# Fourier mixing and a hard-swish layer: folding the first units on VectorE, with later evictions and another order of the first weight pieces

## The chip, the cores and the metric

The kernel runs on one core of a Trainium2 chip. The metric is the device time of one execution, in microseconds (us). TensorE is called PE here, VectorE DVE, ScalarE ACT, GpSimd POOL and SyncE SP, as in the profile. POOL, SP and ACT each have a queue from which DMA transfers are requested; the transfers of all three run on the same 16 DMA engines.

## The reference

```python
# x: (8, 3008, 256), w_in: (256, 2048), w_out: (2048, 256), all float32 or cast to it
X = np.fft.fft(x, axis=1)
X = np.fft.fft(X, axis=2)
t = X.real.astype(np.float32).reshape(8 * 3008, 256)
h = t @ w_in                       # the weights come in as 64-bit floats
g = h * np.clip(h + 3.0, 0.0, 6.0) / 6.0
out = (g @ w_out).astype(np.float32)
```

The weights arrive in double precision. The kernel reads their words and turns them into float32 itself: the exponent through a small matrix product, the mantissa with integer operations, and a product of both.

## The kernel before

The 3008 positions are 47 x 64. A first stage (`unit_columns`, `unit_middle`) is a product over the 47, a second stage (`stage2_half`) one over the 64, and the transform over the 256 columns is folded into w_in (`fold_w_in`). Then come the two products of the layer (`mlp1`, `mlp2`) in chunks of up to 256 positions, with ACT and DVE doing the activation between them. The images are worked on in pairs. Everything after the first pair's start is prepared beside the layer's products, which keep PE busy.

The program order is written out by hand (a manual schedule); each engine runs its instructions in that order, and waits on semaphores.

**The start.** Before the layer can run, the first image goes through the first stage in four units, in the order `FIRST = [0, 1, 3, 2]`. A unit is a block of four slots of 256 columns. It has two halves (`part` 0 and 1): the block itself (tile `xt` of `hb.x`) and its mirrored partner (`hb.xr`). All eight tiles are fetched by POOL's indirect gathers, one after the other (L175, 512 KB each). To *fold* a half is to add and subtract columns j and 256 - j: the cosine columns are the sums, the sine columns the differences, and columns 0 and 128 (the centre) are copied. The result is the tile `y` (two buffers).

For units 0 and 1 DVE subtracts only the sine columns of the first half (`fold_columns`, L203) into a tile `sine`, and PE makes the sums itself by two products per quarter on the unfolded tile (`unit_by_pe`, L355). All other halves are folded by DVE (`fold_all`, L203 and L212), the centre being copied by DVE (L214) or ACT (L209). `unit_columns` (L347, L352) multiplies a folded half by the tables in `F`, four 64-column quarters side by side in the array; `unit_middle` (L335) does column 128. Both halves accumulate into two PSUM tiles `ps` and a slice `pt`.

`evict_first` (L360) copies a unit's four PSUM tiles to `z` on ACT (L365 to L367; the last one of unit 2 on DVE) and requests two stores `zd<-z` (L379) on SP's queue, the last of all on ACT's. `load_g_half` (L447) loads them back, turned, for the second stage.

**The weight pieces** are called 0, 1, 2, ... Piece j goes through `load_w` (the request, L769 and L774, tile `st`), `exponent_a` on ACT (L790, tile `PM`), `exponent_b` on PE (L804, with the matrix in `FI`, into `ex`), `exponent_c` on ACT (L807), `mantissa` on DVE (L815, L816, tile `top`), and `join` on DVE (L824, tile `wi`, or L830 into `G`). Pieces 0 and 1 are two transfers of 256 KB each; 0 is requested on SP's queue behind `FI`, 1 on ACT's queue after unit 0 has been evicted, 2 and 3 on POOL's queue behind the gathers and two tables. `fold_w_in` (L860) multiplies pieces 0 and 1 by the table `C` into `wps`.

`keep_awake` (L887) is a filler: a product of ones and zeros into a PSUM tile that nobody reads, 512 columns wide. There are four at the start and one behind `fold_w_in(0)`. `clear_table` (L917) is a long ACT copy that zeroes half of the table `T`; there are two.

Of the kernel before, what the change touches and what calls it, by code (L numbers as in the profile page):

```python
# [58 lines left out]
def kernel(  # L59
# [141 lines left out]
    def fold_columns(x, y, part, js, eng):  # L201
        far, near = x[0:PX - 1, js, D - 1:P:-1], x[0:PX - 1, js, 1:P]
        eng.tensor_tensor(y[:, js, P + 1:D], *((far, near) if part else (near, far)), op=AL.subtract)  # L203
        return near, far

    def fold_all(x, part, eng, steps=(slice(0, XC),), copy=None):
        y = ypool.tile([PX - 1, XC + 1, D], F32, tag="y", name="y")
        if copy:
            copy(y[:, 0:XC, 0:P + 1:P], x[0:PX - 1, :, 0:P + 1:P])  # L209
        for js in steps:  # L210
            near, far = fold_columns(x, y, part, js, eng)
            eng.tensor_tensor(y[:, js, 1:P], near, far, op=AL.add)  # L212
            if not copy:
                eng.tensor_copy(y[:, js, 0:P + 1:P], x[0:PX - 1, js, 0:P + 1:P])  # L214
        return y
# [93 lines left out]
    def rows(b):  # L309
        return slice(b * PB, b * PB + N1)  # L310
# [21 lines left out]
    def unit_middle(m, part, x, pt, open_, close):  # L332
        for i, h, js, slots, alone in quarters(m, part):
            t = (1 + part) if alone else (5, 7)[part]
            nc.tensor.matmul(pt[h][i * PB:(i + 1) * PB, js], table(t, h), x[rows(h), slots, P:P + 1], start=open_ and not alone, stop=close,  # L335
                             skip_group_check=True)

    def unit_columns(m, part, src, ps, to, fr, open_, close, only=None):
        for i, h, js, slots, alone in quarters(m, part):
            parts = [(to, fr)]  # L340
            if alone and (to.start or 0) <= P < to.stop - 1:
                parts = [(slice(0, P + 1), slice(0, P + 1)), (slice(P + 1, D), slice(P + 1, D))]
            for a, b in parts:
                t = (1 + part + 2 * (a.start > P)) if alone else (0, 6)[part]
                o = ps[h][i * PB:(i + 1) * PB, js, a]
                if only is None:
                    nc.tensor.matmul(o, table(t, h), src[rows(h), slots, b], start=open_ and not alone, stop=close, skip_group_check=True)  # L347
                    continue
                js_, sl = range(js.start, js.stop), range(XC)[slots]
                for jj, ss in zip(js_, sl):  # L350
                    if jj == only:
                        nc.tensor.matmul(ps[h][i * PB:(i + 1) * PB, jj:jj + 1, a], table(t, h), src[rows(h), ss:ss + 1, b],  # L352
                                         start=False, stop=close, skip_group_check=True)

    def unit_by_pe(m, part, x, sine, ps, open_):  # L355
        unit_columns(m, part, x, ps, slice(0, P + 1), slice(0, P + 1), open_, False)
        unit_columns(m, part, x, ps, slice(1, P), slice(D - 1, P, -1), False, False)
        unit_columns(m, part, sine, ps, slice(P + 1, D), slice(P + 1, D), False, False)

    def evict_first(hb, m, ps, pt):  # L360
# [6 lines left out]
        (nc.vector.tensor_copy if k == NM - 1 else nc.scalar.copy)(z[:, 1, :, 0:D], ps[1][0:PX])  # L367
# [391 lines left out]
    def load_w(j):  # L759
# [5 lines left out]
        if kind == "in":  # L765
            c0, c1 = in_columns(n, i)
            for h, cs in enumerate((slice(c0, c1 + P),) if n else (slice(c0, c0 + P), slice(c1, c1 + P))):
                nf = cs.stop - cs.start
                (nc.sync, nc.scalar, nc.gpsimd)[min(j, 2)].dma_start(  # L769
# [113 lines left out]
    def keep_awake(n, ps=None):  # L883
        if ps is None:
            ps = ps_d.tile([P, 2 * TB], F32, tag="d", name="awake")
        for i in range(n):
            nc.tensor.matmul(ps[:], ones[:], Z[:], start=True, stop=True)  # L887
# [65 lines left out]
    mantissa(0)  # L953
    clear_table(1)
    every = slice(0, D)

    def fold_unit(k, part):
        x = (hb.xr if part else hb.x).pop(FIRST[k])
        if k < 2 and part == 0:
            sine = cpool.tile([PX - 1, XC, D], F32, tag="c", name="sine")  # L960
            fold_columns(x, sine, 0, slice(0, XC), nc.vector)
            return x, sine
        steps = (slice(1, XC, 2), slice(0, XC, 2)) if k == NM - 1 and part else (slice(0, XC),)
        return x, fold_all(x, part, nc.vector, steps, nc.scalar.copy if k > 1 else None)
# [338 lines left out]
```

## Time and profile before

| | us |
|---|---|
| runs | 1934.41, 1934.05, 1938.8 |
| median | 1934.41 |
| profiled execution, in all | 1933.92 |
| span of its core, first to last instruction | 1932.2 |
| granted TensorE clock, mean over the span | 0.997 |
| PE busy | 1915.4 |
| DVE busy | 1425.0 |
| ACT busy | 679.3 |
| POOL busy | 1442.7 |

The time of an execution is its span and 1.7 us around it. A row of the timeline gives start, length, engine, line, operation, output and inputs with their shapes, how many instructions are merged, and in brackets how long the engine was idle before and what ended that. A row of the busy time by stretches gives the stretch and its length, then for each engine the busy time and the number of instructions, then the granted clock (1.00 is full speed), the share of the DMA engines' time and GB/s. A row of the groups gives line, engine, operation, forms and count, then the busy time and the mean ns of one, then the idle time before them with what ended it.

### The profile page before, as it was taken

What the parts mean: (1) busy time and instruction counts of PE and PEld (TensorE: products, weight loads), DVE (VectorE), ACT (ScalarE), POOL (GpSimd) and SP (SyncE); (2) the same over time, 40 slices, a digit from 0 to 9 for tenths busy, and PEclk for the clock granted to TensorE, in tenths of its full rate; (3) what the DMA queues carried; (4) which work ended last, traced back from release to release, by engine and by line L of the source; (5) the groups of instructions that cost most, each with busy time, mean ns of one, the idle gap of its engine ahead of it and who ended that gap; (6) DMA issues with size and microseconds to landing.
All of it is one profiled execution on the core that took longest, in us unless ns stands there. A gap on an engine that the chain in (4) does not pass through costs nothing.

```text
span 1932.2 us, 28221 instructions
## 1 busy us (share of the span) xinstructions
PE 1915.4 (99%) x9354; PEld 1650.8 (85%) x9354; DVE 1425.0 (74%) x2752; ACT 679.3 (35%) x1168; POOL 1442.7 (75%) x1653
## 2 busy tenths in 40 slices
PE   8999999999999999999999999999999999999998
PEld 5688888888988888888898888888899888888887
DVE  6877776677777777777787777777778777777777
ACT  6543333333333333333333333333333333333332
POOL 4597888896688778787678877878666667666765
PEclk9999999999999999999999999999999999999999
DMA  8431232311112222121111221121110101101000
GB/s 286 122 87 49 56 83 72 64 44 38 32 33 67 62 53 55 44 54 34 31 36 50 52 55 44 52 53 50 36 28 20 28 17 27 33 14 28 18 21 20
DMA packets 155592, 99.03 MB, mean 51 GB/s; under 512 B 122163, under 2 KB 137246, under 8 KB 155446
## 3 DMA queue, kind: packets, MB, share of 16 engines
q1 hardware_dynamic: 142582, 57.63, 12.4%
q0 software_dynamic: 11168, 38.51, 6.8%
q8 instruction: 73, 1.20, 0.3%
q10 hardware_dynamic: 1696, 1.10, 0.2%
q14 instruction: 73, 0.60, 0.1%
HBM read 59.87 MB, written 37.32 MB: 50 GB/s over the span
## 4 chain that ended last, share of the span: by engine, by line
PE 96%; DVE 2%; ACT 1%; DMA 0%; issue 0%; another core or an unknown queue 0%; SPq 0%; DVEq 0%; ACTq 0%
PE acc L661 57%; PE v L566 17%; PE u L566 16%; PE ps L514 2%; PE acc L641 1%; PE ps L287 1%; DVE a L617 1%; PE spare L860 1%; DVE s L575 0%; ACT t L614 0%; DVE o L722 0%; PE ps L475 0%; DVE u L598 0%; DMA st<-in_moe_w_in_dram 0%; PE wps L860 0%
## 5 line engine op out<-in xcount | busy, mean ns | idle before, releaser
L631 POOL TENSOR_TENSOR c<-a 128x512 f32<-128x512 f32 (+1 forms) x375 | 469.0, 1251 | 360.3 <-PE acc L661 310.5
L661 PE MATMUL acc<-c,G 128*128 128x256 f32 (+1 forms) x3008 | 697.2, 375 | 0.0
L614 ACT ACTIVATE t<-u,half 128x512 f32<-128x512 f32 (+1 forms) x384 | 260.5, 678 | 1144.2 <-DVE u L585 1062.4
L661 PEld LDWEIGHTS acc<-c,G 128*128 128x128 f32 x3008 | 565.3, 190 | 71.5 <-POOL c L631 0.4
L575 DVE SCALAR_TENSOR_TENSOR s<-qn,WN,u 128x256 f32<-128x256 f32 (+1 forms) x768 | 330.2, 471 | 339.3 <-PE u L566 336.7
L661 PE MATMUL acc<-a,G 128*128 128x256 f32 (+1 forms) x2256 | 541.7, 376 | 0.0
L661 PEld LDWEIGHTS acc<-a,G 128*128 128x128 f32 x2256 | 421.0, 189 | 73.6 <-issue 20.2
L566 PE MATMUL v<-q,W 127*128 127x256 f32 (+1 forms) x1536 | 389.2, 375 | 1.6 <-DVE a L617 1.3
L566 PE MATMUL u<-q,W 128*128 128x256 f32 (+1 forms) x1536 | 387.9, 375 | 0.0
L617 DVE SCALAR_TENSOR_TENSOR a<-t,u 128x512 f32<-128x512 f32 (+2 forms) x448 | 263.9, 601 | 102.5 <-ACT t L614 99.4
L566 PEld LDWEIGHTS v<-q,W 127*128 127x128 f32 x1536 | 287.9, 190 | 42.0 <-ACT t L614 2.2
L566 PEld LDWEIGHTS u<-q,W 128*128 128x128 f32 x1536 | 285.8, 190 | 36.9 <-issue 2.4
L631 POOL TENSOR_TENSOR c<-a,c 128x256 f32<-128x256 f32 (+1 forms) x375 | 268.5, 716 | 29.4
L631 POOL TENSOR_TENSOR c<-c,a 128x256 f32<-128x256 f32 (+1 forms) x375 | 268.4, 716 | 29.4
L585 DVE TENSOR_TENSOR u<-s,v 128x512 f32<-128x512 f32 x352 | 245.0, 696 | 38.1 <-DVE s L575 1.9
L617 DVE SCALAR_TENSOR_TENSOR a<-t,v 128x512 f32<-128x512 f32 (+1 forms) x480 | 263.1, 564 | 0.2
L614 ACT ACTIVATE t<-v,half 128x512 f32<-128x512 f32 (+1 forms) x384 | 260.4, 678 | 0.6 <-issue 0.4
L587 DVE TENSOR_TENSOR v<-v,s 128x512 f32<-128x512 f32 x352 | 243.7, 692 | 0.0
L631 POOL TENSOR_TENSOR r<-w,e 128x256 f32<-128x256 f32 (+1 forms) x92 | 88.8, 986 | 3.6
L671 ACT ACTIVATE e<-acc 128x512 f32<-128x512 f32 (+2 forms) x184 | 83.3, 544 | 0.0
L722 DVE STREAM_TRANSPOSE o<-r 128x256 f32<-128x256 f32 (+1 forms) x192 | 72.5, 414 | 0.2
L631 POOL TENSOR_TENSOR w<-w,e 128x512 f32<-128x512 f32 (+1 forms) x46 | 57.5, 1251 | 3.6
(127 smaller groups left out, 773.2 us busy)
## 6 DMA issues: line engine op xcount, KB each, us to landing
out_dram<-o SPq DMA_DIRECT2D x744, 32.0 KB
g<-zd SPq DMA_DIRECT2D x42, 256.0 KB
zd<-z SPq DMA_DIRECT2D x48, 192.0 KB
xt<-in_x_dram POOLq DMA_DIRECT2D x21, 256.0 KB, 3.7
st<-in_moe_w_out_dram POOLq DMA_DIRECT2D x8, 512.0 KB, 6.6
qn<-qd SPq DMA_DIRECT2D x16, 256.0 KB
xt<-in_x_dram POOLq DMA_DIRECT2D x17, 192.0 KB, 4.0
st<-in_moe_w_in_dram POOLq DMA_DIRECT2D x6, 512.0 KB, 4.9
```

What stands on the lines that cost most here:

```text
L287: nc.tensor.matmul(ps[b][h * PB:(h + 1) * PB, 0:n], F[rows(b), 0:PB], y[rows(b), 2 * h:2 * h + n], start=True, stop=not last, skip_group_c ...
L514: nc.tensor.matmul(ps[:, blk, u * P:n].rearrange("p (b k) -> p b k", b=2), g[:, kk, blk * (P + 1):blk * (P + 1) + P], T[:, :, gr, blk, kk, ...
L566: nc.tensor.matmul(ps[:, i, 0:nq], W1[r, blk, f * P:(f + 1) * P], q[r, blk, of:of + nq], start=True, stop=True)
L575: nc.vector.scalar_tensor_tensor(s[:, i, 0:nq], qn[:, of:of + nq], WN[:, f:f + 1], u[:, i, 0:nq], op0=AL.mult, op1=AL.add)
L585: nc.vector.tensor_tensor(u[:], s[:], v[:], op=AL.add)
L587: nc.vector.tensor_tensor(v[:], v[:], s[:], op=AL.subtract)
L614: nc.scalar.activation(t, h, AF.Relu, bias=half[:], scale=scale)
L617: nc.vector.scalar_tensor_tensor(dst, t, 1.0, h, op0=AL.min, op1=AL.mult)
L631: (eng or nc.gpsimd).tensor_tensor(out, in0, in1, op=AL.add)
L661: nc.tensor.matmul(ch.acc[i // 2][:, i % 2, 0:ch.n], G[:, i, fc, :], mv, start=(fc == 0 and i % 2 == 0), stop=(fc == NF - 1), skip_group_c ...
L671: nc.scalar.mul(ch.e[:, k:i + 1, 0:ch.n], ch.acc[i // 2][:, 0:i + 1 - k, 0:ch.n], 1.0 / WS)
L722: nc.vector.transpose(o[:, 0:n // DH, h], ch.r[:, m, h, 0:n].rearrange("p (j i) -> p j i", i=DH))
```

## The change

Every half of every unit is now folded by DVE, in a function `fold_unit` that takes the place of the three before; the centre columns are copied by ACT, except for the first and the last half, where DVE copies them. `unit_by_pe` and the tile `sine` are gone. In each half the narrow products (`unit_middle`) come behind the wide ones, and behind those a filler of 128 columns, except after the very first half and in the last unit. A unit is evicted one unit later: its copies and stores stand behind the first half of the next unit, those of the third unit behind the folding of the last half. DVE copies the last tile of units 3 and 2 (the third and fourth), not of the fourth alone.

Piece 0 is requested first on SP's queue; `FI` goes second on ACT's queue. Piece 1 is requested on SP's queue, behind the stores of the first unit. The exponent products of piece 0 stand ahead of the units on PE, with a filler of 128 columns behind them. After the units there is one more filler, of 256 columns, between the exponent products of pieces 1 and 2, and DVE does the mantissa of piece 2 ahead of the join of piece 1.

```diff
+    def fold_unit(x, part, steps=(slice(0, XC),), copy=nc.scalar.copy, sine=nc.vector):
         y = ypool.tile([PX - 1, XC + 1, D], F32, tag="y", name="y")
+        n = PX - 1
         for js in steps:
+            copy(y[:, js, 0:P + 1:P], x[0:n, js, 0:P + 1:P])
+            far, near = x[0:n, js, D - 1:P:-1], x[0:n, js, 1:P]
+            sine.tensor_tensor(y[:, js, P + 1:D], *((far, near) if part else (near, far)), op=AL.subtract)
+            nc.vector.tensor_tensor(y[:, js, 1:P], near, far, op=AL.add)
         return y
...
-        (nc.vector.tensor_copy if k == NM - 1 else nc.scalar.copy)(z[:, 1, :, 0:D], ps[1][0:PX])
+        (nc.vector.tensor_copy if k > 1 else nc.scalar.copy)(z[:, 1, :, 0:D], ps[1][0:PX])
...
-                (nc.sync, nc.scalar, nc.gpsimd)[min(j, 2)].dma_start(
+                (nc.gpsimd if j > 1 else nc.sync).dma_start(
...
-    def keep_awake(n, ps=None):
-        if ps is None:
-            ps = ps_d.tile([P, 2 * TB], F32, tag="d", name="awake")
+    def keep_awake(n, w=2 * TB):
+        ps = ps_d.tile([P, 2 * TB], F32, tag="d", name="awake")
         for i in range(n):
-            nc.tensor.matmul(ps[:], ones[:], Z[:], start=True, stop=True)
+            nc.tensor.matmul(ps[:, 0:w], ones[:], Z[:, 0:w], start=True, stop=True)
...
-    nc.sync.dma_start(out=FI[:], in_=c_stage1[:, 13 * PB:])
     load_w(0)
     nc.scalar.dma_start(out=F[:], in_=c_stage1[:, 0:8 * PB])
+    nc.scalar.dma_start(out=FI[:], in_=c_stage1[:, 13 * PB:])
...
     mantissa(0)
+    exponent_b(0)
+    keep_awake(1, P)
     clear_table(1)
-    unit = fold_unit(0, 0)
     for k, m in enumerate(FIRST):
         ps, pt = first_banks(m)
-        x, y = unit
-        if k == 0:
-            unit_middle(m, 0, x, pt, True, False)
-        if k < 2:
-            unit_by_pe(m, 0, x, y, ps, True)
-        else:
-            unit_columns(m, 0, y, ps, every, every, True, False)
-        if k == 0:
-            exponent_b(0)
-            exponent_c(0)
-        else:
-            unit_middle(m, 0, x, pt, True, False)
-        x, y = fold_unit(k, 1)
-        unit_middle(m, 1, x, pt, False, True)
-        if k < NM - 1:
-            unit_columns(m, 1, y, ps, every, every, False, True)
-            unit = fold_unit(k + 1, 0)
-        else:
-            for j in range(2):
-                unit_columns(m, 1, y, ps, every, every, False, True, only=j)
-            join(0)
-        evict_first(hb, m, ps, pt)
-        if k == 0:
-            nc.scalar.copy(zero_slot(hb), first_slot[PB:PX, 0:D])
-            load_w(1)
+        end = k == NM - 1
+        for part, tiles in enumerate((hb.x, hb.xr)):
+            x = tiles.pop(m)
+            if end and part:
+                y = fold_unit(x, 1, (slice(1, XC, 2), slice(0, XC, 2)), copy=nc.vector.tensor_copy)
+                evict_first(hb, FIRST[k - 1], *before)
+                unit_middle(m, 1, x, pt)
+                for j in range(2):
+                    unit_columns(m, 1, y, ps, only=j)
+                join(0)
+                continue
+            y = fold_unit(x, part, copy=nc.scalar.copy if k + part else nc.vector.tensor_copy)
+            unit_columns(m, part, y, ps)
+            unit_middle(m, part, x, pt)
+            if k + part and not end:
+                keep_awake(1, P)
+            if k == part == 0:
+                exponent_c(0)
+            if part == 0 and k > 0 and not end:
+                evict_first(hb, FIRST[k - 1], *before)
+            if k == 1 and part == 0:
+                nc.scalar.copy(zero_slot(hb), first_slot[PB:PX, 0:D])
+                load_w(1)
+        before = ps, pt
+    evict_first(hb, m, *before)
     load_g_half(hb, 0)
     load_g_half(hb, 1)
...
     exponent_c(1)
+    keep_awake(1, TB)
     exponent_a(2, (1,))
+    mantissa(2)
     join(1)
-    mantissa(2)
```

More of the change, by code (lines that the diff above doesn't have):

```diff
@@ L330, in quarters, with unit_middle @@
                     yield i, h, slice(1, 2), slice(XC - 1, XC) if part == 0 else slice(0, 1), True
[L332 removed]
+    def unit_middle(m, part, x, pt):
         for i, h, js, slots, alone in quarters(m, part):
             t = (1 + part) if alone else (5, 7)[part]
[L335 to L353 removed]
@@ L355, in unit_by_pe @@
[L355 to L358, printed above, removed]
+            nc.tensor.matmul(pt[h][i * PB:(i + 1) * PB, js], table(t, h), x[rows(h), slots, P:P + 1],
+                             start=part == 0 and not alone, stop=part == 1, skip_group_check=True)
@@ L953 @@
     mantissa(0)
+    exponent_b(0)
+    keep_awake(1, P)
     clear_table(1)
[L955 to L964, printed above, removed]
```

24 lines of the change are left out of this document (13 added, 11 removed).

## The prediction

> **What bounds the kernel now.** I read the page first, then the busy time by stretches, then the chain that ended last in the stretch which the edit touches, then the timeline of that stretch.
>
> ```profile
> span 1932.2 us, 28221 instructions
> PE 1915.4 (99%) x9354; PEld 1650.8 (85%) x9354; DVE 1425.0 (74%) x2752; ACT 679.3 (35%) x1168; POOL 1442.7 (75%) x1653
> ...
> PE 96%; DVE 2%; ACT 1%; DMA 0%; issue 0%; another core or an unknown queue 0%; SPq 0%; DVEq 0%; ACTq 0%
> ```
>
> TensorE (PE) is busy nearly throughout and makes up 96% of the chain that ended last. The stretches say where it is not. Their columns are PE, weight load, VectorE (DVE), ScalarE (ACT), GpSimd (POOL), then the granted TensorE clock, the DMA share and GB/s.
>
> ```profile
> 2.00:24.00 22.00, 18.96 (x191) 9.05 (x190) 12.02 (x24) 13.14 (x25) 11.66 (x15) 0.89 1.00 341
> 24.00:26.00 2.00, 2.00 (x5) 1.63 (x6) 0.79 (x2) 0.70 (x2) 0.00 (x0) 0.54 0.11 39
> 12.17:15.58 3.41, 2.66 (x44) 1.29 (x43) 1.20 (x3) 1.95 (x6) 3.40 (x6) 1.00 0.97 347
> 15.58:19.00 3.42, 1.96 (x44) 1.54 (x41) 3.07 (x5) 2.00 (x10) 0.30 (x1) 1.00 1.00 292
> 19.00:22.41 3.41, 3.41 (x38) 1.96 (x35) 2.71 (x7) 1.40 (x5) 0.00 (x0) 0.50 1.05 349
> 22.41:25.82 3.41, 3.41 (x21) 2.12 (x14) 0.69 (x1) 0.59 (x2) 0.00 (x0) 0.50 0.49 184
> 25.82:29.23 3.41, 2.59 (x10) 1.32 (x9) 2.19 (x4) 3.17 (x5) 0.00 (x0) 1.00 0.37 94
> 43.60:1923.00 1879.40, 1877.12 (x9083) 1628.44 (x9084) 1392.54 (x2682) 652.09 (x1120) 1420.94 (x1619) 1.00 0.18 46
> ```
>
> From 43.60 to 1923 PE is idle for 1879.40 - 1877.12 = 2.3 us. The edit adds and removes nothing there, so it can only move the moment at which that stretch begins. All it can win or lose lies in the first 43.6 us. Two resources fill those: the DMA engines (share 1.00 at 341 GB/s up to 24 us) and, from 19.00 to 25.82, a PE at half clock.
>
> The chain inside the start, in order of time (start, length, what):
>
> ```profile
> 22.15 1.81 PE ps L352 x16
> 23.96 2.86 PE wps L860 x8
> 26.82 0.86 PE awake L887 x2
> 27.68 0.45 PE ex L804 x2
> 28.13 0.02 issue
> 28.15 0.58 ACT ex L807
> 28.73 0.67 ACT PM L790
> 29.40 0.04 issue
> 29.45 0.38 PE ex L804
> 29.82 1.73 PE wps L860 x8
> ```
>
> The listed chain goes through the last products of the folded units (L352), the first weight product (L860) and the filler (L887). Beside it runs a second one that is almost as long, through the landing of the second weight piece:
>
> ```profile
> 25.89 2.09 ACT L790 ACTIVATE PM<-st,bias 128x512 uint8<-128x512 int16 x3 [1.30 <-DMA st<-in_moe_w_in_dram]
> 28.15 0.58 ACT L807 ACTIVATE ex<-ex 128x512 int32<-128x512 f32 x1 [0.17 <-PE ex L804]
> 28.76 0.69 DVE L824 TENSOR_TENSOR wi<-top,ex 128x512 f32<-128x512 f32 x1 [1.11 <-ACT ex L807]
> ```
>
> ACT waits for that piece until 25.89, then works without a gap to 25.89 + 2.09 = 27.98, and then waits only 0.17 us for PE. So this is the number that matters most: **if PE came out of the units any amount earlier, and the piece landed when it does now, the start would gain 0.17 us and no more.** What decides is when the second piece lands.
>
> **The change part by part.**
>
> *All eight unit halves folded by VectorE, filler behind each.* The rows that price it:
>
> ```profile
> 11.56 0.94 POOL L175 DMA_INDIRECT xt<-in_x_dram,IT  x1 [0.30 <-issue]
> ...
> xt<-in_x_dram,IT POOLq DMA_INDIRECT x9, 7.7
> ...
> L203 DVE TENSOR_TENSOR y<-xt 111x508 f32<-111x508 f32 x5 | 3.4, 686 | 3.6 <-PE ps L347 2.4 <-DMA xt<-in_x_dram,IT 1.0 <-issue 0.2
> L212 DVE TENSOR_TENSOR y<-xt 111x508 f32<-111x508 f32 x5 | 3.4, 679 | 0.0
> ...
> 17.18 1.10 PE L347 MATMUL ps<-y,F 47*64 47x512 f32 x12 [1.46 <-ACT y L209]
> 17.55 0.68 DVE L212 TENSOR_TENSOR y<-xt 111x508 f32<-111x508 f32 x1
> ```
>
> It adds two additions on DVE (units 0 and 1, first half), 2 x 0.68 = 1.4 us, and takes from PE the 16 + 16 products that worked on x directly. A half unit is then 1.3 us of DVE and some 1.4 us of PE (1.10 for the four wide products, 0.3 for the narrow ones), for seven halves 9 us after about 7.5 us: DVE would be through by 17. It cannot be, because the last half arrives with the last gather, at 11.56 + 7.7 = 19.3 us. Its two half-width steps of copy, subtraction and addition (1.7 us) end near 21, its products near 22 at full clock. Before, they ended at 23.96. So the units end 1 to 2 us earlier, and by the argument above 0.17 us of that counts. Six fillers of 128 columns cost 0.86/4 = 0.21 us each and one of 256 costs 0.43; each stands where PE waits for DVE, ACT or the piece, so I take them at nothing; without that cover the last, in front of the second weight product, would cost its 0.43.
>
> *First exponent products ahead of the units, evictions one unit later.* Two more rows:
>
> ```profile
> 7.00 1.45 ACT L790 ACTIVATE PM<-st,bias 128x512 uint8<-128x512 int16 x2 [1.29 <-DMA st<-in_moe_w_in_dram]
> 8.36 2.73 ACT L917 COPY T<-Z 64x3072 f32<-64x3072 f32 x1
> ```
>
> PE now waits for ACT until 7.00 + 1.45 = 8.45 before the first half; DVE has that half folded near 9, so nothing is lost. The centre columns of the second half now come from ACT instead of DVE, behind the table clear (to 11.09) and the exponent step (0.58): near 11.9, where DVE had them at 10.5. PE stands from about 10.4 to 11.9, and may get its half clock there, from 12.17 to 15.58 instead of from 19.00. That costs the units up to 1.7 us, in a stretch where they have 2 us and more before the last gather: their end is 22 to 23. In ACT's queue the evictions stand behind the centre copies of the next half and ahead of the one after it, which can so wait for 1.4 us of copies; the same slack covers it. The last unit's stores leave 1 to 2 us earlier, and what they feed (the g loads) is not last: PE reaches that stage only behind the second weight product, which starts at 29.82.
>
> *Piece order.* The rows:
>
> ```profile
> 13.61 0.58 ACT L807 ACTIVATE ex<-ex 128x512 int32<-128x512 f32 x1 [2.51 <-remote]
> 13.92 0.40 ACTq L769 DMA_DIRECT2D st<-in_moe_w_in_dram  x1
> 14.35 0.55 ACTq L769 DMA_DIRECT2D st<-in_moe_w_in_dram  x1
> 15.31 10.03 SPq L379 DMA_DIRECT2D zd<-z  x7
> ...
> zd<-z SPq DMA_DIRECT2D x7, 64.2 KB
> ```
>
> The first piece is requested one DMA earlier (0.4 us), since the exponent matrix FI goes to ACT's queue; that queue's later steps start 0.4 us later and POOL's is not touched. What ACT and DVE do on the piece is gone by 9, so nothing follows. The second piece moves from ACT's queue (issued 13.92 and 14.35, used at 25.89, 11 us later) to SP's, behind the two stores of the first unit. These start no earlier than that unit's evictions; from 15.31 plus two issues, I put the request at 15.5 to 17, some 2 us later than now. All the queues together, though, are one backlog that runs at 341 GB/s until 24 us, and the bytes are the same. The piece lands now with the very last of it. Behind it in SP's queue there will be the four stores of units 1 and 2, 4 x 64.2 KB = 257 KB, 0.75 us of the measured rate. So one end is a landing 0.75 us earlier. The other end is that it is again last and waits for the two stores ahead of it too, 128 KB or 0.4 us, with another 0.6 us for a late request: 1.0 us later. I take 0.5 us earlier, since the backlog ends at the same time whichever order it has, and this order no longer puts the piece at its end.
>
> The Trainium skill ("DMA: Bandwidth & Descriptors", Queues, rings and completion order) says that each DMA engine goes round the queues that have work, packet by packet; by that, giving up a queue of its own costs the piece turns, which speaks for the later end. No row of this trace separates the two, since both queues end together.
>
> *Mantissa of piece 2 ahead of the join of piece 1.* DVE idles 1.11 us before that join (row 28.76 above), and the two steps take 0.43 + 0.69; they fit, and leave DVE up to 1.1 us earlier behind it. PE's second weight product covers most of that: 0.1 us.
>
> **Sum.** 0.17 + 0.5 + 0.1 = 0.8 us off the span, 1932.2 to 1931.4. The profiled execution took 1933.92 in all, 1.7 us more than its span, and the median of the runs, 1934.41, is 0.5 above that. 1931.4 + 1.7 + 0.5 = **1933.6 us**.
>
> **The rivals.**
>
> *The clock is halved later instead of earlier (slower).* The rows show the rule: after a stretch of 3.4 us with 1.96 us of PE the clock went to 0.50, for 6.8 us; after 2.66 and 2.59 us it stayed at 1.00. The edge lies between. With the units done early, the first weight product and its filler slip out of the stretch 25.82 to 29.23 and what is left there is waiting for the second piece: 4 exponent products (0.4 us each with their waits), a filler of 0.43, a rest of the 0.86 filler, about 2.3 us. If that falls under the edge, the second weight product and what follows (29.82 on) run at half clock for 3.41 us and lose 1.7 us, all of it on the path: 1933.6 + 1.7 = 1935.3, and 1937.0 if it takes two stretches. For it: the count is close. Against it: the fillers stand there, and the limits of the stretches may fall otherwise. 0.28.
>
> The Trainium skill ("TensorE: Matmul & The Clock Gate", HAM oscillation) says that only idle gaps over about 3.4 us bring the half clock; by that this rival would have no chance and the small fillers no use. The trace disagrees: the gap of 1.46 us in the row 17.18 was enough.
>
> *The second piece comes later (slower).* 1.0 us late gives 1934.4 - 0.3 + 1.0 = 1935.1. It decides if the request slips past 17 us. ACT's unexplained 2.51 us at 13.61 speaks for it, since the same wait now stands in front of the evictions. 0.10.
>
> *The piece lands with the bulk.* DMA share falls to 0.11 at 24.00; were the piece there at 24.3, 1.5 us earlier, PE would just be ready, and the time 1934.4 - 1.8 = 1932.6. 0.11.
>
> *Nothing moves*: the piece is last again, 1934.2. It lies inside the forecast's own range, 1932.9 to 1934.6; together 0.42.
>
> **How the numbers follow.** 0.3% is 5.8 us, about what a measurement of this kernel can tell from no change. None of the cases reaches it: to win 5.8 us the piece would have to land at 20, to lose it at 31.7 or the clock to be halved for 11.6 us on the path. I leave 0.03 for faster and 0.06 for slower, against what I have not seen (a wait on SP's or ACT's queue that the trace of before does not have). The range takes in the larger gain and both slower rivals: 1931.5 to 1937.0.
>
> **What would show it.** Right: the wait of ACT's exponent step for the second piece ends near 25.4; the last unit products end by 22 to 23; PE is without gaps from about 43 us and its stretch to the end is as long as before. Wrong: that wait ends past 26.5; a stretch after 26 us has clock 0.50; or PE has more than 2.3 us of idle time behind the start, which would mean that the edit reaches further than I say.

## The result, and the profile after

The changed kernel takes 1940.9 us (median of seven runs, 1936.3 to 1942.6), the kernel before 1935.43 beside it (eight runs, 1934.05 to 1938.8): ratio 1.0025, 95% interval 1.0013 to 1.0036. Ratios here and below are taken over all the runs that count, not from the medians. The forecast was 1933.6 with a range to 1937.0, so the time lies 3.9 us above the range. (An eighth run of 2890 us, at a mean granted clock of 0.65, is left out.) The profiled execution took 1940.9 with a span of 1939.1, 6.9 more than before.

The page of the changed kernel, the lines that answer to those shown of before:

```profile
span 1939.1 us, 28192 instructions
PE 1921.7 (99%) x9336; PEld 1655.2 (85%) x9336; DVE 1428.7 (74%) x2756; ACT 679.3 (35%) x1169; POOL 1442.8 (74%) x1653
...
PE 95%; DVE 2%; ACT 1%; POOL 1%; issue 0%; DMA 0%; ACTq 0%; DVEq 0%; SPq 0%; POOLq 0%
```

PE has 6.3 us more busy time in 18 fewer instructions: the instructions got longer. The busy time by stretches of the changed kernel says where (PE, weight load, DVE, ACT, POOL, granted clock, DMA share, GB/s):

```profile
8.47:11.88 3.41, 2.07 (x26) 0.88 (x30) 3.00 (x5) 2.54 (x4) 2.80 (x3) 1.00 0.98 375
11.88:15.29 3.41, 3.41 (x32) 1.94 (x24) 1.29 (x3) 0.28 (x3) 3.41 (x5) 0.50 1.04 353
15.29:18.71 3.42, 2.19 (x14) 0.68 (x17) 1.28 (x2) 1.62 (x5) 0.79 (x2) 0.50 0.93 285
18.71:22.12 3.41, 3.41 (x37) 2.76 (x30) 1.60 (x3) 0.27 (x3) 0.00 (x0) 0.50 1.01 333
22.12:25.53 3.41, 2.81 (x24) 2.10 (x24) 1.06 (x4) 1.23 (x5) 0.00 (x0) 0.50 0.66 208
25.53:28.95 3.42, 3.15 (x31) 1.62 (x31) 2.67 (x8) 0.54 (x3) 0.00 (x0) 0.50 0.00 0
28.95:32.36 3.41, 3.41 (x27) 2.14 (x24) 1.36 (x3) 0.98 (x4) 0.00 (x0) 0.50 0.16 39
32.36:35.77 3.41, 3.13 (x13) 1.86 (x12) 2.35 (x5) 2.96 (x5) 0.00 (x0) 1.00 0.29 56
50.36:1929.80 1879.44, 1877.14 (x9082) 1628.12 (x9083) 1394.19 (x2682) 652.43 (x1120) 1420.97 (x1619) 1.00 0.18 46
```

The closed stretch is as long as before (1879.44 against 1879.40) and begins at 50.36 instead of 43.60: 6.8 of the 6.9 us. Ahead of it PE ran at half clock for six stretches on end, 11.88 to 32.36, 20.5 us, where before there were two (19.00 to 25.82). Note two rows of it: from 11.88 and from 18.71 PE is listed as busy all of 3.41 us, and still the clock does not come back. Behind the row from 28.95, which is just as busy, it does.

The timeline of the changed kernel shows what the halving hangs on and what it makes of the rest:

```profile
7.56 2.74 ACT L904 COPY T<-Z 64x3072 f32<-64x3072 f32 x1
10.96 1.13 PE L334 MATMUL ps<-y,F 47*64 47x512 f32 x8 [0.85 <-ACT y L205]
...
15.59 0.61 ACT L355 COPY z<-ps 112x512 f32<-112x512 f32 x1
16.23 0.40 ACT L967 COPY xt<-first_slot 48x256 f32<-48x256 f32 x1
16.66 0.69 DVE L207 TENSOR_TENSOR y<-xt 111x508 f32<-111x508 f32 x1 [3.18 <-ACT xt L967]
16.91 1.99 PE L334 MATMUL ps<-y,F 47*64 47x512 f32 x8 [1.23 <-ACT y L205]
17.61 1.17 SPq L757 DMA_DIRECT2D st<-in_moe_w_in_dram  x2
...
30.81 2.74 PE L848 MATMUL wps<-wi,C 128*128 128x256 f32 x8
31.57 0.42 DVE L803 TENSOR_SCALAR top<-st 128x512 int32<-128x512 int32 x1
50.36 1.99 PE L848 MATMUL spare<-wi,C 128*128 128x256 f32 x8 [0.27 <-DVE wi L812]
```

The second half of the first unit waits 0.85 us for its centre copy, which stands on ACT behind the table clear (to 10.30) and the exponent step; behind that the clock is halved. A half's wide products then take 1.99 us instead of 1.13 (rows 16.91 and 10.96). The second half of the second unit waits 1.23 us for its centre copy, behind ACT's copies of the first unit's PSUM tiles. DVE waits too, 3.18 us, for ACT's copy of the zero slot (row 16.23) before it can fold the third unit. The units end at 30.8 instead of 23.9. The second weight piece is used without a wait (row 31.57: no bracket), so its landing no longer decides. In the chain that ended last the fillers now stand between the units' products, at 0.73 us each:

```profile
23.30 1.97 PE ps L334 x6
25.27 0.34 PE pt L329 x9
25.61 0.73 PE awake L874 x2
26.34 1.90 PE ps L334 x6
```

### The profile page after: what moved, and what is told of

Read it like the earlier page. It is cut to its first block, busy times and chain, and to the rows that moved or that the text cites. A ratio compares the mean times of both kernels' runs of the same rounds, so it can differ in the third digit from the quotient of the medians.

```text
span 1939.1 us, 28192 instructions
## 1 busy us (share of the span) xinstructions
PE 1921.7 (99%) x9336; PEld 1655.2 (85%) x9336; DVE 1428.7 (74%) x2756; ACT 679.3 (35%) x1169; POOL 1442.8 (74%) x1653
## 4 chain that ended last, share of the span: by engine, by line
PE 95%; DVE 2%; ACT 1%; POOL 1%; issue 0%; DMA 0%; ACTq 0%; DVEq 0%; SPq 0%; POOLq 0%
PE acc L649 55%; PE v L554 16%; PE u L554 16%; PE ps L502 2%; PE acc L629 1%; PE ps L281 1%; DVE a L605 1%; PE ps L334 1%; PE spare L848 1%; DVE s L563 0%; ACT t L602 0%; POOL c L619 0%; DVE o L710 0%; DVE u L586 0%; PE ps L463 0%
```

## The experiments

Three theories at first. *Clock*: the lost clock is the whole difference. *Order*: the halves wait for ACT's late evictions and copies, whatever the clock. *Filler*: the new fillers stand on the chain. All later ratios are to the kernel before, run on the same chip. Four chips were used, and the kernel before had medians of 1934.4 to 1935.7 on them, so times from different chips compare to 1 to 2 us only.

**Gaps filled.** A wide filler ahead of the first half and behind it.

```diff
-    keep_awake(1, P)
+    keep_awake(1)
...
-            if k + part and not end:
-                keep_awake(1, P)
+            if not end:
+                keep_awake(1, P if k + part else 2 * TB)
```

> The changed kernel, with the filler ahead of the first half 512 columns wide instead of 128, and a filler of 512 behind the first half, where there was none: PE's two gaps before 11.88 us are filled. Clock theory (the half clock that began at 11.88 is the loss): the clock stays at 1.00 past 12 us, the units end by 24, PE's closed stretch begins at 43 to 44.5 instead of 50.4, the time is 1933.5 to 1936. Order theory (the halves wait for ACT's late evictions, whatever the clock): the ends move by less than 1 us, 1940. Filler theory (fillers take PE time that the path needs): 0.5 to 1.5 us slower than the changed kernel.

1940.51 us, ratio 1.0028 (1.0016 to 1.0039): no gain, and 4.5 us above the range of the clock theory. Timeline of this kernel:

```profile
16.11 1.09 PE L334 MATMUL ps<-y,F 47*64 47x512 f32 x8 [1.57 <-ACT y L205]
```

The clock now outlived the first gap, but the next one, behind the evictions, halved it at 17.54 instead, for 13.65 us. The place of the loss moved as the clock theory says; the time didn't follow, since the next gap did the same. (That this gap is the reason was shown only later, by the kernel with the clock held.)

**No unit fillers.** All six 128-column fillers taken out.

```diff
-    keep_awake(1, P)
...
-            if k + part and not end:
-                keep_awake(1, P)
```

> The changed kernel without its six fillers of 128 columns. Filler theory: 3 to 4 us faster, about 1937, since five of them cost 0.73 us each at half clock and stand on the chain. Clock theory: the clock is halved at 12 us or before and stays so for as long or longer; the fillers' time is won back but the half clock keeps the loss, 1937 to 1941. Order theory: 1940, the halves wait for ACT as before.

1938.11, ratio 1.0022 (1.0013 to 1.0031), not told apart from the changed kernel's (the medians lie 2.8 us apart, but were not taken side by side). The clock was halved from 17.75 for 10.24 us. Without the fillers most of the loss is still there, so they are not its cause.

**Piece order alone**, in the kernel before.

```diff
-                (nc.sync, nc.scalar, nc.gpsimd)[min(j, 2)].dma_start(
+                (nc.gpsimd if j > 1 else nc.sync).dma_start(
...
-    nc.sync.dma_start(out=FI[:], in_=c_stage1[:, 13 * PB:])
     load_w(0)
     nc.scalar.dma_start(out=F[:], in_=c_stage1[:, 0:8 * PB])
+    nc.scalar.dma_start(out=FI[:], in_=c_stage1[:, 13 * PB:])
```

> The kernel before, with the order of the requests alone changed (piece 0 first, FI on ACT's queue, piece 1 on SP's behind the first unit's stores). All three theories: within 1 us of the kernel before; the wait for piece 1 ends between 25 and 26.5. More than 3 us slower would mean that the request order carries the loss.

1934.91, ratio 1.0002 (0.9993 to 1.0011): the order of requests costs nothing that can be measured. The expected end of the wait for the second piece can't be seen here, since the units ended after it had landed, at 26.38. Its profiled execution happened to have the half clock for 17.07 us, from 11.82, behind this gap:

```profile
11.09 1.81 PE L347 MATMUL ps<-y,F 47*64 47x512 f32 x8 [1.24 <-issue]
```

So the units of the kernel before are open to the same loss. Its runs between 1932 and 1940 may come from where the stretches of 3.41 us fall on its gaps; a trace of one of its slower runs, which would show it, was not taken.

**Quarter warm-up.** Why did a busy PE not get its clock back? The kernel before, its four fillers at the start replaced by four rounds of quarter products on 47 rows, the shape of the units' own products.

```diff
-    keep_awake(4)
+    for n in range(4):
+        for i in range(2):
+            for h in range(2):
+                nc.tensor.matmul(quarters_awake[h][i * PB:(i + 1) * PB], ones[rows(h), 0:PB],
+                                 Z[rows(h)].rearrange("p (a b) -> p a b", a=2), start=True, stop=True,
+                                 skip_group_check=True)
```

> The kernel before, with the four fillers at its start replaced by four rounds of four quarter products (47 rows, 64 columns, 512 moving columns), the shape of the unit products, back to back with nothing to wait for. Clock theory in its form by cells (a product that fills 73% of the array does not bring the full clock): no full clock at 5 us, and none until the first weight product at 24 us or later; units at half clock, 3 to 6 us slower than before. Clock theory in its form by time (dense products of any shape bring it): full clock at 5 to 9 us, within 1 us of before.

1938.70, ratio 1.0020 (1.0011 to 1.0029). Its timeline:

```profile
1.61 7.10 PE L896 MATMUL awake<-Z,ones 47*64 47x512 f32 x32 [1.61 <-DVE ones L891]
8.85 1.97 PE L347 MATMUL ps<-xt,F 47*64 47x258 f32 x16
28.33 3.78 PE L860 MATMUL wps<-wi,C 128*128 128x256 f32 x8
```

The clock came first at 33.28, behind the first whole-array weight products. The profile holds no record of the clock ahead of that (a view by stretches prints 1.00 for such time), but the lengths tell: up to there everything has its half-clock length; the products of row 8.85 take 1.97 us, and 1.07 in the next kernel. PE had hardly been idle from 1.61 on.

**Full cells.** The same with all 64 rows of each quarter.

```diff
-                nc.tensor.matmul(quarters_awake[h][i * PB:(i + 1) * PB], ones[rows(h), 0:PB],
-                                 Z[rows(h)].rearrange("p (a b) -> p a b", a=2), start=True, stop=True,
+                nc.tensor.matmul(quarters_awake[h][i * PB:(i + 1) * PB], ones[h * PB:(h + 1) * PB, 0:PB],
+                                 Z[h * PB:(h + 1) * PB].rearrange("p (a b) -> p a b", a=2), start=True, stop=True,
```

> The kernel before with its four whole-array fillers at the start replaced by four rounds of four quarter products, as in the quarter warm-up, but each with all 64 rows of its quarter instead of 47: the four together fill every cell of the array. Cells theory (each stretch of 3.41 us is judged by how much of the array works for how long, and dense quarter products of 47 rows, at 4*47*64/128^2 = 0.73 of the cells, fall short once the clock is halved): the clock is full from about 5 us on, as with whole-array fillers, and the time is 1933 to 1936. Shape theory (a product that is smaller than the array does not count, however many run side by side): no full clock before 28 to 33 us, as in the quarter warm-up, and 1938 to 1940.

1934.1 in the one run (before: 1935.14). Its timeline:

```profile
1.61 6.50 PE L896 MATMUL awake<-Z,ones 64*64 64x512 f32 x32 [1.61 <-DVE ones L891]
8.66 1.07 PE L347 MATMUL ps<-xt,F 47*64 47x258 f32 x16
25.54 0.38 PE L804 MATMUL ex<-PM,FI 128*128 128x512 f16 x1 [1.60 <-ACT PM L790]
```

Full clock from 7.36. So what decides is neither the shape of the products nor the busy time: the rows, and with them the number of the array's cells at work, are all that differs. It was halved once more, for 3.41 us from 27.84, behind PE's wait for the second weight piece (row 25.54).

**54 rows**, between the two, 0.84 of the cells (`h * PB:h * PB + 54`).

> The kernel before with the quarter warm-up at 54 rows of each quarter, 4*54*64/128^2 = 0.84 of the array's cells, between the 0.73 at which the clock never came before the first whole-array products and the 1.00 at which it came from 7.4 us on. Cells theory with one edge near 0.40 of full work, as the halved stretches suggest: at half clock dense products of 54 rows are worth 0.42, the clock comes as at 64 rows, 1932 to 1936. If the edge for coming back lies between 0.42 and 0.50, or only products of all 64 rows count, it does not come before 28: 1937 to 1940.

The clock came, at 6.77. Dense products of 47 rows at half clock are worth 0.73 x 0.5 = 0.37 of full work, those of 54 rows 0.42; the edge for coming back lies between the two, as the cells theory had it. The time, 1938.64 in the one run, missed: the clock was lost again in the units, at 13.60, behind this stretch of its windows:

```profile
10.19:13.60 3.41, 1.57 (x22) 0.87 (x17) 2.90 (x7) 2.03 (x1) 3.10 (x5) 1.00 1.02 405
```

**Clock held.** The changed kernel with fillers wide enough for every gap.

```diff
-    keep_awake(1, P)
+    keep_awake(1)
...
-            if k + part and not end:
-                keep_awake(1, P)
+            if not end:
+                wide = {(0, 0): 1, (1, 0): 2, (2, 0): 1}.get((k, part))
+                keep_awake(wide or 1, 2 * TB if wide else P)
```

> The changed kernel with wider whole-array fillers where PE stands: 512 wide before the first half and behind it, two of 512 behind the first half of the second unit, one of 512 behind the first half of the third. Clock theory: the gap of 1.57 us that halved the clock with the gaps filled is covered, the clock stays full until the units' end, which then comes near 24 to 24.5 instead of 30.9; PE's closed stretch starts near 44.5 instead of 50.36, and the time is 1935 to 1936.5. Order theory (the halves wait for ACT's late evictions whatever the clock): units end after 27, time 1937 to 1940. Filler theory (each filler on the chain costs its length): 2.5 us more of fillers, 1941 or more.

1933.76, ratio 0.9996 (0.9987 to 1.0005), its runs within 0.7 us; better than the 1935 to 1936.5 expected. Fillers 2176 columns wider in all, 3.7 us at 0.86 us for 512, took the ratio from 1.0025 to 0.9996, 5.6 us (7 by the medians). The order and filler theories fall as accounts of the loss: ACT's copies and evictions stand where they stood, and there are more fillers. Timeline of this kernel:

```profile
13.75 1.98 PE L874 MATMUL awake<-Z,ones 128*128 128x512 f32 x4
24.20 1.99 PE L848 MATMUL wps<-wi,C 128*128 128x256 f32 x8
43.39 1.99 PE L848 MATMUL spare<-wi,C 128*128 128x256 f32 x8 [0.27 <-DVE wi L812]
```

The closed stretch begins at 43.39, and the clock was full from 6.68 to 1928.

**Before, clock held.** The kernel before, with a filler of 512 ahead of its second unit and two ahead of its third (`if k in (1, 2): keep_awake(k, ps[0])`).

> The kernel before with one whole-array filler of 512 ahead of its second unit and two ahead of its third, where PE stands 0.75 and 1.46 us. Clock theory: the clock is full through all units, which end near 22 instead of 23.96; the second weight piece (ACT's wait for it ended at 25.89) then sets the start, so that 1932.5 to 1934 come out and the runs lie closer together than the 1932.3 to 1939.4 of the kernel before. Order and filler theories: the fillers stand on the chain and delay the units by 0.2 to 0.5 each, 1934.5 to 1936.

1932.96, ratio 0.9992 (0.9983 to 1.0001). Not shown to be faster, and its runs still lie 4.9 us apart, which the clock theory did not expect. The units ended at 21.9, and then the clock was lost behind the wait for the second piece, 27.72 to 34.54.

**ACT out of the way.** The changed kernel with all centre copies on DVE, the zero slot ahead of the evictions.

```diff
-            y = fold_unit(x, part, copy=nc.scalar.copy if k + part else nc.vector.tensor_copy)
+            y = fold_unit(x, part, copy=nc.vector.tensor_copy)
...
+            if k == 1 and part == 0:
+                nc.scalar.copy(zero_slot(hb), first_slot[PB:PX, 0:D])
             if part == 0 and k > 0 and not end:
                 evict_first(hb, FIRST[k - 1], *before)
             if k == 1 and part == 0:
-                nc.scalar.copy(zero_slot(hb), first_slot[PB:PX, 0:D])
                 load_w(1)
```

> The changed kernel with every centre copy of the folds on DVE, and ACT's copy of the zero slot ahead of the evictions instead of behind them: no half of a unit waits for an eviction on ACT any more. The small fillers stay. Order theory: PE's waits of 0.85, 1.23 and 0.60 us for ACT's copies are gone, 2.7 us in all, and at half clock the units still end near 28: 1938 to 1939. Clock theory: without the waits one half is 1.1 us of quarter products and 0.2 us of filler in about 1.6 us, over 0.6 of the array's full work, so that the clock is never halved: units end near 22 to 23, PE's closed stretch starts near 43.5 to 44.5, and the time is 1933.5 to 1935. Filler theory: 1940 to 1941 as after, since the fillers stay.

1933.39, ratio 0.9998 (0.9989 to 1.0007); one run of eleven at 1939.89. Without ACT's waits the clock holds through the units with the small fillers. So the loss goes when the gaps are filled, and goes when they are not made: ACT's copies make the gaps, as the order theory had it, but the cost of the gaps is the clock (at half clock that theory expected 1938 to 1939). Timeline of this kernel:

```profile
21.14 1.99 PE L848 MATMUL wps<-wi,C 128*128 128x256 f32 x8
25.39 0.43 DVE L803 TENSOR_SCALAR top<-st 128x512 int32<-128x512 int32 x1 [3.41 <-DMA st<-in_moe_w_in_dram]
26.21 0.38 PE L792 MATMUL ex<-PM,FI 128*128 128x512 f16 x1 [2.22 <-ACT PM L778]
43.88 1.99 PE L848 MATMUL spare<-wi,C 128*128 128x256 f32 x8 [0.39 <-DVE wi L812]
```

This is the forecast's picture at last: the units done early, and everybody waiting for the second piece until 25.39. (By the measure that is worked out below, its stretches in the units come to 0.46 to 0.53 of full work, over the edge, though not the over 0.6 that was expected.) Ending the units 2.75 us earlier than the kernel before (21.14 against 23.89) brought nothing: 43.88 against 43.63.

**Second piece early.** That kernel, with the second piece on POOL's queue right behind `C`.

```diff
-                (nc.gpsimd if j > 1 else nc.sync).dma_start(
+                (nc.gpsimd if j > 0 else nc.sync).dma_start(
...
+    load_w(1)
     load_t(0, queue=nc.gpsimd)
...
-                load_w(1)
```

> The kernel with ACT out of the way, and the second weight piece requested on POOL's queue right behind C, ahead of T and of the two pieces of w_out, instead of on SP's queue behind the first store. Second-piece theory: there the units end at 21.2, PE stands 2.2 us for the exponent of the second piece, which landed at 25.4, and the clock is halved once more at 27.1 because of that wait; requested at about 13 the piece lands near 20 to 21, the wait and the halving are gone, and the next thing late is the first transfer of g back from DRAM, which landed up to 30.5: PE's closed stretch starts near 42.8 instead of 43.88, time 1931.5 to 1932.5. Rival (the landing doesn't set the start, everything behind it is late on its own): 1933 to 1934 as without it.

Ratio 0.9999 (0.9987 to 1.0011), but in two groups: five runs at 1932.1 to 1932.2, as the second-piece theory expected, and six at 1937.7 to 1939.9. The profiled one was of the upper group, its clock halved from 11.49 for 20.48 us behind a gap of 1.04 us.

**Before, both**: the held kernel before with the same early piece.

> The kernel before with the three fillers that held its clock and with the second weight piece requested on POOL's queue right behind C instead of on ACT's. Second-piece theory: its units ended at 21.9 with the fillers, the first piece-2 work on DVE waited until 25.77; with the landing near 20 to 21 that wait goes, PE's closed stretch starts near 43 and the time is 1931.5 to 1932.5. Rival: 1932.5 to 1934 as with the fillers alone.

1932.81, ratio 0.9993 (0.9984 to 1.0002), runs from 1931.9 to 1936.6: not told apart from the fillers alone. The expected 1931.5 to 1932.5 was reached by three runs of eleven.

**Second wait filled.** The kernel with ACT out of the way, four fillers of 512 instead of one behind the first weight products (`keep_awake(4)`).

> The kernel with ACT out of the way, and four whole-array fillers of 512 instead of one behind the first weight products, where PE stood 2.2 us for the second piece. Nothing else moves. Clock theory: the wait itself stays, but the halving at 27.1 that followed it goes (3.41 us at half clock, of which PE's work costs about 0.5 to 1 us): PE's closed stretch starts near 43.3 instead of 43.88, the time is 1932.4 to 1933.2, and the runs lie within about 1 us instead of 1932.7 to 1939.9. Filler theory: the fillers end 0.2 after the exponent's inputs are there, 1933.4 to 1934.

1941.21, ratio 1.0033 (1.0020 to 1.0045): a miss by 8 us. Timeline of this kernel:

```profile
13.48 0.17 DVE L205 COPY y<-xt 111x8 f32<-111x8 f32 x1 [1.66 <-PE pt L329]
14.90 1.09 PE L334 MATMUL ps<-y,F 47*64 47x512 f32 x8 [0.77 <-DVE y L208]
```

The clock went at 16.77, in the units, ahead of the edited place: a half that started at 13.61 with ACT out of the way starts at 14.90 here. Why DVE comes later there is not shown. The edit stands behind the units in program order; but the two kernels also ran on different chips (11 and 2), and no run tells a chance of the chip from an effect of the edit.

**Both of these with the clock held**: fillers of 512 ahead of the first half and behind the first halves of units one and two.

```diff
-    keep_awake(1, P)
+    keep_awake(1)
...
-            if k + part and not end:
-                keep_awake(1, P)
+            if not end:
+                keep_awake(1, P if part or k > 1 else 2 * TB)
```

> The kernel with the second piece early, whose times fell into two groups (1932.1 to 1932.2 and 1937.7 to 1939.9), with wider whole-array fillers in the early units: 512 ahead of the first half and behind the first halves of the first and second unit, where its profiled run stood 1.04 us and lost the clock at 11.49 for 20.48 us. Clock theory: the upper group is the runs that lost the clock, so all runs come out at 1932.0 to 1933.0. Rival (the two groups come from the piece's landing or from something else that varies): the groups stay, median 1932 to 1938 with runs above 1937; and if fillers only cost, 1 to 2 us are added to each group.

1932.15, ratio **0.9983 (0.9974 to 0.9992)**, all eleven runs between 1931.8 and 1933.2: the only version whose interval lies below 1, so the only one shown to be faster than the kernel before, by 0.17%. Its timeline:

```profile
22.81 0.42 DVE L803 TENSOR_SCALAR top<-st 128x512 int32<-128x512 int32 x1
30.34 1.13 PE L455 MATMUL ps<-T,g 128*128 128x128 f32 x8 [1.05 <-DMA g<-zd]
42.66 1.99 PE L848 MATMUL spare<-wi,C 128*128 128x256 f32 x8 [0.27 <-DVE wi L812]
```

The second piece is worked on at 22.81 without a wait, and what is late next is the load of g, as expected.

> The kernel with the second wait filled, all of whose runs were at 1940.4 to 1942.4, with the same wider whole-array fillers in the early units: 512 ahead of the first half and behind the first halves of the first and second unit. There the clock was lost at 16.8 in the units, ahead of the place that had been edited. Clock theory: the clock is held, the units end near 22 to 23, and what the filled wait was to show shows now: no halving behind the units either, 1932.4 to 1933.5, the runs within 1 us. Rival (the three fillers behind the first weight products cost 6 to 8 us by themselves, by a way that the profile does not show): 1940 or more as before.

1934.09, ratio 0.9993 (0.9984 to 1.0002): 7 us less than without the early fillers, runs within 0.6 us, and no half clock in its profile. So the runs without those had most likely all lost the clock in the units, as their profiled one did. It stays 0.6 above the expected range; the four fillers end late, which fits (timeline of this kernel):

```profile
24.31 3.60 PE L874 MATMUL awake<-Z,ones 128*128 128x512 f32 x8
24.53 2.10 ACT L778 ACTIVATE PM<-st,bias 128x512 uint8<-128x512 int16 x3 [1.35 <-DMA st<-in_moe_w_in_dram]
27.75 0.59 PE L792 MATMUL ex<-PM,FI 128*128 128x512 f16 x2
```

ACT's three steps of 0.7 us begin at 24.53, the first is done near 25.2; PE takes it up at 27.75. Both held versions ran on another chip than those without the early fillers; each ratio is to the kernel before on its own chip.

All profiles together (us; half clock ahead of the closed stretch, start of the first weight products and of the closed stretch in the profiled execution, which can be far from the median run; median of the runs). "Half clock" leaves out the start of each trace, before the full clock first comes, except for the quarter warm-up. The kernel before has its median of the first three runs here.

| kernel | half clock | weight products | closed stretch | median |
|---|---|---|---|---|
| before | 6.83 | 23.89 | 43.63 | 1934.4 |
| changed | 20.48 | 30.81 | 50.36 | 1940.9 |
| gaps filled | 13.65 | 28.78 | 48.76 | 1940.5 |
| no unit fillers | 10.24 | 26.26 | 45.90 | 1938.1 |
| piece order alone | 17.07 | 26.38 | 46.41 | 1934.9 |
| quarter warm-up | to 33.28 | 28.33 | 49.57 | 1938.7 |
| full cells | 3.41 | 21.09 | 43.78 | 1934.1 |
| 54 rows | 17.07 | 28.23 | 48.23 | 1938.6 |
| clock held | 0 | 24.20 | 43.39 | 1933.8 |
| before, clock held | 6.83 | 21.92 | 45.91 | 1933.0 |
| ACT out of the way | 3.41 | 21.14 | 43.88 | 1933.4 |
| second piece early | 20.48 | 29.20 | 49.36 | 1937.7 |
| before, both | 0 | 24.20 | 43.36 | 1932.8 |
| second wait filled | 13.65 | 26.58 | 49.84 | 1941.2 |
| early piece, held | 0 | 22.05 | 42.66 | 1932.2 |
| second wait, held | 0 | 22.48 | 43.86 | 1934.1 |

## Why the prediction was wrong

*What bounds the kernel* held: the closed stretch is the same, and only its beginning moved.

*The step that failed* is the last of the exponent and eviction part: PE "may get its half clock there, from 12.17 to 15.58 instead of from 19.00. That costs the units up to 1.7 us". The place was right (11.88, behind the gap of 0.85 us). The term was mis-sized: 20.48 us instead of 3.41, and some 7 us instead of 1.7. And the sum carried it at nothing, since the units were to have 2 us of slack there; the loss was larger than the slack, and the closed stretch began 6.8 us later. The forecast took for granted that the clock comes back by itself. The rule under it, PE's busy time (1.96 us of 3.41 halves, 2.66 does not), was the wrong measure: the changed kernel's stretches from 11.88 and 18.71 have 3.41 of 3.41 at half clock and bring nothing back.

What decides can be worked out from the records. The clock's states between the start and the closed stretch last 3.41, 6.83, 10.24, 13.65, 17.07 or 20.48 us, whole multiples of 3.41, so take it that the clock is set anew every 3.41 us. Count for each product the time that it takes at full clock (0.86 us for 512 columns of 32 bits, 0.22 of 16 bits, by the chain's rows 26.82 and 27.68 in the prediction), times the share of the array's cells that it uses, spread over the time in which it is listed; add this up for a stretch and divide by its 3.41 us. Of the 188 stretches that end within the first 44 us of the sixteen traces, those under 0.37 were followed by half clock and those above it by full clock, whichever clock they had themselves. (Moving the limits of the stretches by 0.15 us shifts this: between 0.35 and 0.39 both then occur. So the edge is good to about 0.02.) The measure was found in these same traces; the one run that was forecast from it is the one with 54 rows, whose clock came as forecast. By that measure:

- A half's four quarter products are worth 0.86 x 4 x 47 x 64 / 128^2 = 0.63 us. The changed kernel's stretch from 8.47 holds one half and most of the next (10.96 to 12.09), with a rest of filler 0.34 of full work: halved. The kernel before has 0.46 in its stretch from 8.76 and kept the clock.
- At half clock such products can fill a stretch with 0.73 x 0.5 = 0.37 at most, the edge itself, and any gap takes them under it. The changed kernel's five stretches from 11.88 to 28.95 come to 0.21 to 0.30. So PE can be listed as busy throughout and not get out, until the weight products (whole array, 0.5) come at 30.8 and lift the stretch from 28.95 to 0.38. That is the trap that the forecast missed.
- The edit itself thinned the work. In the first halves of units 0 and 1 PE used to stream 258 + 254 + 254 = 766 columns per quarter where it now streams 512. The prediction booked that as time won; by this measure it was also work that kept the clock. How much it did by itself no run shows: the piece order alone kept the 766 columns and lost the clock all the same, behind its gap of 1.24 us (0.36 in the stretch ahead of 11.82).

*Earlier units gain 0.17 us and no more*: this fits what the runs show, but the changed kernel never got there. With full cells and with ACT out of the way the units ended 2.8 us earlier, and the closed stretch began 0.15 and 0.25 us later than before (each with one halving behind the units).

*Piece order*: the request came at 17.61, not 15.5 to 17 (at 16.33 with ACT out of the way). The landing half a microsecond earlier is not shown. In the new order ACT's wait for the piece ended at 25.39 (ACT out of the way) and 24.53 (second wait, held), in the old one at 25.89 (before), 25.76 (before, clock held) and 24.72 (full cells): both scatter by more than the term, so that 25.39 beside the forecast 25.4 is luck. The order alone made 1.0002. The later end, for which the Trainium skill's turn-taking of queues ("DMA: Bandwidth & Descriptors", Queues, rings and completion order) spoke, isn't seen.

*The mantissa's new place* (0.1 us) can't be seen beside the rest. *Fillers at nothing* was wrong at half clock (0.73 us each on the chain), but small beside the rest: without them the ratio is 1.0022 instead of 1.0025.

*The first rival*, the clock halved behind the units, is a real mechanism: full cells, ACT out of the way and the held kernel before show it at 27 to 28. In the changed kernel the units' end had slipped past it. The range took in a halving only there, for one or two stretches. Its sign of being wrong did come true, though from another cause: the changed kernel has the half clock in the stretches from 25.53 and 28.95. Of the signs of being right only the length of the closed stretch held. The difference, 0.25%, lies within the 0.3% of the chances; the range was too narrow for six stretches in the units.

## What to carry to other kernels

Where PE works on part of its array, read the granted clock beside the busy time, stretch by stretch, and count cells, not busy time: in these traces work that filled under 0.37 of a stretch was followed by half clock, and dense products on 73% of the cells did not win the full clock back. A few wide whole-array fillers in the gaps cost less than they saved here, and with the clock held through the units the changed kernel's versions agree from run to run (within 0.6 to 1.4 us, where the runs of the kernel before lay 3 to 8 us apart). The kernel before with its three fillers did not get there: its runs still lay 4.7 and 4.9 us apart. And before a stage is made faster, look whether it is what keeps the clock up.

## What the hardware showed unexpectedly

- One edge for losing and regaining the clock, near 0.37 of full work over 3.41 us (good to about 0.02), in 188 stretches. The fillers, products of ones and zeros, are counted in full there, and the edge comes out sharp.
- The Trainium skill ("TensorE: Matmul & The Clock Gate", Part 1: The HAM clock gate (the "warmup" mystery)) has the full clock come after one busy window of about 3.4 us. With whole-array products the traces agree (PE starts at 1.6 us and has the full clock from 4.6 to 7.5). With quarter products on 47 rows they don't: PE hardly stood from 1.61 to 28.33 and had none of it.
- The same page says that the window runs freely, and that what a start costs varies from run to run. The traces agree: with the same four fillers at the start, the kernel before has the full clock from 5.34, and with its clock held from 7.23. That would also make two groups of times out of one kernel, as in the one with the early second piece (1932.1 to 1932.2 and 1937.7 to 1939.9; with its clock held, all at 1931.8 to 1933.2), but no trace of its faster group was kept to show it.
- Open: what makes PE's gaps that the profile puts down to issue (1.24 us at 11.09 in the piece order alone), and what makes DVE late in the second wait filled.
